# A contiguous buffer for the weights' shift, and another order of the first units' work, in a gated attention block with an MLP

## The chip, the cores and the metric

The kernel runs on one core of one Trainium2 chip. A core has five engines that each take their own instructions in order: TensorE (PE, matrix products; its weight loads are listed as PEld), VectorE (DVE), ScalarE (ACT), GpSimd (POOL) and SyncE (SP, which here only issues transfers). Sixteen DMA engines move data between the memory (DRAM) and the core's own memory (SBUF). Matrix products land in PSUM banks. The metric is the time of one execution on the device, in microseconds (us).

## The reference

Two blocks in a row. The first is a linear attention with a forget gate (4 batches, 8 heads, 768 steps, head size 48); the second is a layer norm and an MLP with ReLU and a residual (width 384, hidden 1536).

```python
f = 1.0 / (1.0 + np.exp(-f_logit))
for t in range(S):
    state = f[:, :, t, :, None] * state + np.einsum('bhd,bhe->bhde', k[:, :, t], v[:, :, t])
    y[:, :, t] = np.einsum('bhd,bhde->bhe', q[:, :, t], state)
...
x = np.ascontiguousarray(attn_out.transpose(0, 2, 1, 3)).reshape(B, S, H * D)
mu = np.mean(x, axis=-1, keepdims=True)
var = np.mean((x - mu) ** 2, axis=-1, keepdims=True)
xn = (x - mu) / np.sqrt(var + 1e-06) * g_ln
ch = np.maximum(xn @ w_ch1, 0.0) @ w_ch2
return (x + ch).astype(np.float32)
```

The MLP's weights arrive as 64-bit floats, all else as 32-bit floats. The kernel makes 32-bit floats of the weights itself.

## The kernel before

**Units and stages.** The 768 steps are cut into 12 units of 64 steps, all batches and heads together. A unit n has a list of attention stages, written a{n}.stage: gates (PE transposes f into a PSUM bank, ACT takes the sigmoid), after and upto (DVE scans with running products of the gates), kx (PE transposes k), k and q (DVE multiplies by the scans' results; q also transposes on PE), scores (PE), causal (DVE masks them), values (PE, and ACT copies the result to x), kt (PE transposes k back, ACT copies), chunk and state (the update of the state), stats and norm (DVE, with POOL for the root), turn (PE transposes the normed x, ACT multiplies by the gain into xt). For unit 0 most stages are done for two pairs of batches apart, with a 0 or 1 behind the name. Transposes and MLP products share four PSUM banks in turn; a bank is taken again when its last reader is done.

**The MLP.** Unit 0's first matrix product is done in steps h00 (first half of the tokens) and h01 (second half), six each; a step takes 256 of the 1536 hidden columns, 12 matmul instructions and a relu on ACT. So step i of h00 or h01 needs the weight piece i. For later units, and for the second product, the steps are named m{n}.

**The weights.** Both matrices are cut into six pieces each (w1: 256 columns of three row blocks; w2: two row blocks), 768 KB apiece as 64-bit words. A piece goes through four tokens of the list:

- f (line 513): SP issues its transfer into one of two "words" buffers.
- r (line 524): ACT reads the words twice, into "upper" (the high word, scaled; line 533) and into half of "units" (the low word; line 534).
- c (line 539): DVE clips "upper" (line 544) and shifts its bits by three (line 546). The shift writes straight to the piece's place in w1 or w2. In w1 that place is three runs of 256 elements out of rows of 1536; in w2 it is one run.
- w (line 550): ACT writes the signs into the other half of "units" (line 556), POOL adds "units" to the shifted words in place (line 557).

**The order.** START, a list of tokens written out by hand, gives the order in which the instructions of units 0 to 2 (and parts of 3 to 5) are put out; UNIT does the same for each later unit. As each engine works in order, the list sets the order on every engine and on the queues. Beside those above there are: l (load of f, q, k or v of a unit from SP's queue; L is the same from ACT's queue; a digit at the end is one of the two pairs of batches; a load of a pair is two transfers of 96 KB), p and P (splits into halves for transposing transfers, sent from POOL's or SP's queue), x (such a transfer), t, u and U (sums of weights, on DVE or POOL), and d (line 568: a matrix product of the identity with itself, into a bank that nobody reads).

The list is worked off by `run`:

```python
def run(plan):
    for token in plan.split():
```

Of the kernel before, what the change touches and what calls it, by code (L numbers as in the profile page):

```python
# [10 lines left out]
I32 = mybir.dt.int32  # L11
# [4 lines left out]
ALU = mybir.AluOpType  # L16
# [284 lines left out]


START = """
a0.gates0 l0q0 l0f1 f a0.after0 a0.carried l0k1 a0.upto0 l0k0 a0.gates1 a0.kx0 l0q1 f l0v0 l0v1 a0.after1 r c a0.upto1 a0.kx1 a0.k0 f a0.q0 a0.q1 w a0.scores0 a0.causal0 a0.k1 r f c w a0.values0 a0.kt a0.scores1 l1f a0.stats0 a0.causal1 r c d a0.norm0 l1q a0.chunk w a0.values1 a0.turn0 a0.stats1 r d a1.gates h00 c a0.norm1 a1.after w h00 a0.turn1 f f h00 r l1k a0.state h01 h01 h01 f a1.upto a1.kept c h00 a1.q w l1v r a1.kx a1.carried a1.k a1.scores a1.causal c r l2f w h00 f a1.values h01 a1.stats c l2k a2.gates f h01 r a1.kt h01 l3f l2q h00 a1.norm a1.turn a2.after f a2.kx w c a2.k P3f0 p3f1 a1.chunk w r l3k f r c a2.upto m1 a1.state f m1 m1 w P3k1 c m1 P3k0 w l3q a2.kept m1 t m1 r r x3f c l2v m1 w a3.gates a2.q L4f x3k a3.after c m1 a2.carried P3q1 a2.kt P3q0 w L4k a2.scores m0 P4f1 a2.causal m0 a2.values U a3.k P3K0 a2.stats u P4k1 a2.chunk m0 p4k0 x3q m0 U m0 a2.state a2.norm l4q a2.turn p3K1 a3.kept a3.upto L3v m0 P4f0 u l5f m2 a3.q t u x4f m2 m2 p4q0 P4q1 a3.kt a3.carried a3.scores a3.causal u t a4.gates x4k m2 m1 u a4.after u m2 m2 P5f0 p5f1 s2 a3.values a3.stats a3.norm l5k m1 U x4q P5k0 a3.chunk P5k1 m1 a4.upto a4.q l6f u l4v m2 l5v x5f m1 a4.k a3.turn a3.state u m2 P4K1 l5q m2 m2 a4.kept m2 u a5.gates p4K0 m2 U m2 y3
"""
UNIT = """
a{n}.kt a{n}.carried p{p}f1 a{o}.after a{n}.scores m{m} a{n}.causal m{m} m{m} m{m} P{o}q0 m{m}
# [8 lines left out]
def kernel(  # L316
# [19 lines left out]
    nc = tc.nc  # L336
    B, H, S, D = q.shape
    P = 128
# [38 lines left out]
    stage = changing.enter_context(tc.tile_pool(name="stage", bufs=2))  # L377
# [11 lines left out]
    for name in "fqk":  # L389
        t = consts.tile([P, G, H, 64], FP32, name=f"{name}raw")  # L390
# [120 lines left out]
    fetched, opened, clipped = [], [], []  # L511
# [27 lines left out]
    def clip():  # L539

        if not opened:
            return
        upper, units, to, name, r, w = opened.pop(0)
        nc.vector.tensor_scalar(out=upper, in0=upper, scalar1=-INF, scalar2=INF, op0=ALU.max,
                                op1=ALU.min)
        nc.vector.tensor_scalar(out=to.bitcast(I32), in0=upper.bitcast(I32), scalar1=3,
                                scalar2=None, op0=ALU.logical_shift_left)
        clipped.append((upper, units, to))

    def write():  # L550

        if not clipped:
            return
        upper, units, to = clipped.pop(0)
        signs = units.bitcast(F16).rearrange("p r (f two) -> p two r f", two=2)[:, 1]
        nc.scalar.activation(out=signs, in_=upper, func=AF.Copy)
        nc.gpsimd.tensor_tensor(out=to.bitcast(I32), in0=to.bitcast(I32), in1=units, op=ALU.add)

# [529 lines left out]
    def run(plan):  # L1090
        for token in plan.split():
# [8 lines left out]
            elif kind == "m":  # L1100
                if token not in running:
                    running[token] = mlp(int(rest))
                next(running[token])
            elif kind in "lL":
                queues = (nc.scalar if kind == "L" else nc.sync,)
                if rest[-1].isdigit():
                    load(int(rest[:-2]), rest[-2], (int(rest[-1]),), queues)
                else:
                    load(int(rest[:-1]), rest[-1], engines=queues)
            elif kind in "pP":  # L1110
                split(int(rest[:-2]), rest[-2], int(rest[-1]),
                      nc.sync if kind == "P" else nc.gpsimd)
            elif kind == "x":
                transfer(int(rest[:-1]), rest[-1])
            elif kind == "h":
                if token not in running:
                    running[token] = first_half(int(rest[0]), int(rest[1]))
                next(running[token])
            elif kind == "s":
                sums(int(rest))  # L1120
            elif kind == "y":
                if FIRST <= int(rest) < NU:
                    sums_of_x(int(rest))
            else:
                {"r": read, "c": clip, "w": write, "f": fetch, "t": mix, "d": idle,
                 "T": lambda: mix(nc.gpsimd), "u": mix_step,
                 "U": lambda: mix_step(nc.gpsimd)}[token]()
# [3 lines left out]
    for m in range(3, NU):  # L1131
# [4 lines left out]
        if m == NU - 2:  # L1136
# [5 lines left out]
                                    op=ALU.min)  # L1142
            nc.vector.tensor_scalar(out=small, in0=least_one, scalar1=LEAST, scalar2=None,
                                    op0=ALU.is_lt)
# [37 lines left out]
```

## Time and profile before

| | us |
|---|---|
| median of 3 runs | 434.26 |
| lowest, highest | 433.57, 434.93 |
| the profiled execution, its own time | 433.42 |
| its span, first to last instruction | 431.6 |
| PE idle in the span | 19.0 |

The granted TensorE clock is 1.00 in every stretch of the profile. In rows of the timeline, the first number is the start in us from the span's start, the second the duration in us; then engine, line, operation, what is written and what is read, shapes and types, how many instructions were merged, and in brackets the idle time before them with what ended it. A name such as SPq or ACTq is the engine's instruction queue, where transfers are issued. In rows by stage, a stretch is followed by the busy time of PE, PEld, DVE, ACT and POOL, the granted clock, the share of the DMA engines' time that was busy, and GB/s.

### The profile page before, as it was taken

How to read it: one execution, taken by the hardware profiler on the slowest of the kernel's cores; microseconds unless marked ns; L12 is line 12 of the kernel's file. 1: busy time of each engine (PE TensorE's matmuls, PEld its weight loads, DVE VectorE, ACT ScalarE, POOL GpSimd, SP SyncE). 2: the span in 40 equal slices, each digit the busy share in tenths (PEclk: the TensorE clock that was granted, in tenths of full speed). 3: DMA queues.
4: the chain of work that ended last, by engine and by line, in shares of the span. 5: the costliest groups of instructions: out<-in, count | busy, mean ns of one | idle time of the engine just before them, and what ended most of it. 6: DMA issues, size and time to landing. Idle time of an engine off the chain costs nothing.

```text
span 431.6 us, 12917 instructions
## 1 busy us (share of the span) xinstructions
PE 412.6 (96%) x5421; PEld 385.8 (89%) x5421; DVE 322.9 (75%) x505; ACT 227.7 (53%) x376; POOL 118.1 (27%) x153
## 2 busy tenths in 40 slices
PE   2799999999999999999999999999999999999995
PEld 1689987668779999989999999999999999999995
DVE  5679757684787879869879879879879879665561
ACT  2597888564252574563573573564673552351320
POOL 3355343421032115016116016016016015012021
PEclk9999999999999999999999999999999999999999
DMA  7999998969677697797697797698695781301001
GB/s 159 242 238 198 224 263 236 183 161 237 166 185 156 179 215 179 191 208 178 179 223 187 186 226 173 167 212 202 163 245 139 171 150 45 92 2 28 12 9 33
DMA packets 167839, 71.68 MB, mean 166 GB/s; under 512 B 151760, under 2 KB 157840, under 8 KB 167776
## 3 DMA queue, kind: packets, MB, share of 16 engines
q1 hardware_dynamic: 153248, 55.56, 59.1%
q0 software_dynamic: 3632, 11.85, 7.7%
q10 hardware_dynamic: 10896, 3.40, 4.2%
q8 instruction: 44, 0.72, 0.7%
q14 instruction: 19, 0.16, 0.1%
HBM read 28.31 MB, written 23.59 MB: 120 GB/s over the span
## 4 chain that ended last, share of the span: by engine, by line
PE 94%; SPq 1%; DMA 1%; DVE 1%; ACT 1%; issue 1%
PE pp L1040 32%; PE bx L940 11%; PE by L940 10%; PE po L1021 7%; PE ph L1011 7%; PE ph L889 4%; PE bz L940 4%; PE shared L760 3%; PE py L746 3%; PE py L796 3%; PE bw L940 2%; PE tr L654 2%; PE xp L875 2%; PE bv L940 2%; PE shared L834 2%; DMA kraw<-in_k_dram 1%
## 5 line engine op out<-in xcount | busy, mean ns | idle before, releaser
L951 ACT ACTIVATE h<-h 128x512 f32<-128x512 f32 x45 | 28.4, 631 | 42.2 <-DVE h L948 33.2
L1040 PE MATMUL pp<-mixed,h 128*128 128x192 f32 x240 | 42.3, 326 | 0.0
L1040 PE MATMUL pp<-w,h 128*128 128x192 f32 x240 | 40.8, 326 | 0.0
L1040 PE MATMUL pp<-mixed,s 128*128 128x192 f32 x240 | 40.6, 326 | 0.0
L1040 PEld LDWEIGHTS pp<-mixed,s 128*128 128x128 f32 x240 | 39.3, 190 | 0.0
L1040 PEld LDWEIGHTS pp<-mixed,h 128*128 128x128 f32 x240 | 39.1, 190 | 0.0
L1040 PEld LDWEIGHTS pp<-w,h 128*128 128x128 f32 x240 | 38.8, 190 | 0.3
L877 ACT ACTIVATE xt<-xp,gain 128x128 f32<-128x128 f32 x72 | 20.1, 380 | 30.7 <-PE xp L875 30.6
L948 DVE TENSOR_TENSOR h<-h,bx 128x512 f32<-128x512 f32 x36 | 24.6, 683 | 15.3 <-PE bx L940 15.3
L427 ACT COPY Kplanes<-kh 128x1024 uint16<-128x1024 uint16 x18 | 18.2, 1046 | 32.6 <-DVE kh L708 27.3
L1021 PE MATMUL po<-w,h 128*128 128x384 f32 x96 | 32.9, 490 | 0.0
L662 DVE TENSOR_TENSOR_SCAN after<-gates,ends 128x1040 f32<-128x1040 f32 (+1 forms) x13 | 28.8, 2216 | 4.8 <-ACT gates L691 3.1
L1011 PE MATMUL ph<-xt,w 128*128 128x256 f32 x144 | 31.9, 380 | 0.0
L1011 PEld LDWEIGHTS ph<-xt,w 128*128 128x128 f32 x144 | 27.2, 190 | 4.2
L673 DVE TENSOR_TENSOR_SCAN upto<-gates,starts 128x1040 f32<-128x1040 f32 (+1 forms) x13 | 30.5, 2349 | 0.4
L940 PE MATMUL bx<-y,v 128*128 128x128 f32 x216 | 28.5, 275 | 0.0
L1021 PEld LDWEIGHTS po<-w,h 128*128 128x128 f32 x96 | 17.7, 190 | 10.7
L940 PEld LDWEIGHTS bx<-y,v 128*128 128x128 f32 x216 | 26.3, 192 | 0.0
L822 POOL TENSOR_SCALAR rstd<-mv 128x2 f32<-128x2 f32 (+1 forms) x13 | 8.0, 615 | 66.4 <-DVE mv L820 66.2
L427 ACT COPY fplanes<-fraw 128x1024 uint16<-128x1024 uint16 x18 | 18.8, 1053 | 9.1 <-DMA kraw<-in_k_dram 4.2
L427 ACT COPY kplanes<-kraw 128x1024 uint16<-128x1024 uint16 x18 | 18.1, 1044 | 6.6 <-DMA kraw<-in_k_dram 5.0
L1040 PE MATMUL pp<-w,s 128*128 128x192 f32 x120 | 21.1, 326 | 0.0
(166 smaller groups left out, 934.0 us busy)
## 6 DMA issues: line engine op xcount, KB each, us to landing
w_0words<-in_moe_w_ch_dram SPq DMA_DIRECT2D x7, 768.0 KB, 6.1
kraw<-in_k_dram SPq DMA_DIRECT2D x44, 96.0 KB, 4.8
v<-in_v_dram SPq DMA_DIRECT2D x44, 96.0 KB, 3.9
Khalves<-Kplanes POOLq DMA_DIRECT2D x16, 256.0 KB, 3.6
fhalves<-fplanes POOLq DMA_DIRECT2D x14, 256.0 KB, 4.2
kraw<-in_q_dram SPq DMA_DIRECT2D x36, 96.0 KB, 3.2
khalves<-kplanes SPq DMA_DIRECT2D x11, 256.0 KB, 2.5
qhalves<-qplanes SPq DMA_DIRECT2D x10, 256.0 KB, 3.8
```

The costliest lines, as they stand in the source:

```text
L427: nc.scalar.copy(out=to, in_=src)
L662: nc.vector.tensor_tensor_scan(out=at["after"].rearrange(flat)[:, c0:c1][:, ::-1], data0=gt[:, c0 + 1:c1 + 1][:, ::-1], data1=ends.rearran ...
L673: nc.vector.tensor_tensor_scan(out=at["upto"].rearrange(flat)[:, c0:c1], data0=gt[:, c0:c1], data1=starts.rearrange(flat)[:, c0:c1], initi ...
L746: nc.tensor.matmul(py[half(b ^ r), r, e * D:(e + 1) * D], lhsT=qh[head_rows(r), 2 * e + b], rhs=kept[head_rows(r), b, e], start=e == 0, st ...
L877: nc.scalar.mul(out=xt[:, m, g * P:(g + 1) * P], in_=pt[:, m], mul=gain[:, m:m + 1])
L889: nc.tensor.matmul(ph[:, j], lhsT=w1[:, m, (i + j) * P:(i + j + 1) * P], rhs=xt[:, m, tokens], start=m == 0, stop=m == KD - 1)
L940: nc.tensor.matmul(banks[bank][:, i], lhsT=right[:, i * P:(i + 1) * P], rhs=left, start=new and i == 0, stop=True, skip_group_check=True)
L948: nc.vector.tensor_tensor(out=out[to], in0=out[to], in1=bank, op=op)
L951: nc.scalar.activation(out=out[to], in_=out[to] if bank is None else bank, func=AF.Relu)
L1011: nc.tensor.matmul(ph[:, j], lhsT=w1[:, m, (i + j) * P:(i + j + 1) * P], rhs=xt[:, m], start=m == 0, stop=m == KD - 1)
L1021: nc.tensor.matmul(po, lhsT=h[:, i, g * P:(g + 1) * P], rhs=w2[:, i], start=i == 0, stop=i == KF - 1)
L1040: nc.tensor.matmul(pp, lhsT=a[:, i], rhs=b[:, i], start=i == 0, stop=i == KH - 1)
```

## The change

The shift writes to a tile "body" of its own, one buffer of 128 x 768 words, and POOL reads it from there:

```diff
@@ clip
-        nc.vector.tensor_scalar(out=to.bitcast(I32), in0=upper.bitcast(I32), scalar1=3,
-                                scalar2=None, op0=ALU.logical_shift_left)
-        clipped.append((upper, units, to))
+        body = stage.tile([P, r, w], I32, tag="body", bufs=1, name=f"{name}body")
+        nc.vector.tensor_scalar(out=body, in0=upper.bitcast(I32), scalar1=3, scalar2=None,
+                                op0=ALU.logical_shift_left)
+        clipped.append((upper, units, body, to))
@@ write
-        upper, units, to = clipped.pop(0)
+        upper, units, body, to = clipped.pop(0)
...
-        nc.gpsimd.tensor_tensor(out=to.bitcast(I32), in0=to.bitcast(I32), in1=units, op=ALU.add)
+        nc.gpsimd.tensor_tensor(out=to.bitcast(I32), in0=body, in1=units, op=ALU.add)
```

START is replaced by another order of nearly the same tokens: 256 in place of 251. Five are d (seven in place of two), two u became U, and ten transfers changed their queue. In the file each list is one line; here the beginnings are broken into several, up to where both have named h00 four times and h01 three times:

```diff
-a0.gates0 l0q0 l0f1 f a0.after0 a0.carried l0k1 a0.upto0 l0k0 a0.gates1 a0.kx0 l0q1 f
-l0v0 l0v1 a0.after1 r c a0.upto1 a0.kx1 a0.k0 f a0.q0 a0.q1 w a0.scores0 a0.causal0
-a0.k1 r f c w a0.values0 a0.kt a0.scores1 l1f a0.stats0 a0.causal1 r c d a0.norm0 l1q
-a0.chunk w a0.values1 a0.turn0 a0.stats1 r d a1.gates h00 c a0.norm1 a1.after w h00
-a0.turn1 f f h00 r l1k a0.state h01 h01 h01 f a1.upto a1.kept c h00 a1.q w l1v r a1.kx
-a1.carried a1.k a1.scores a1.causal c r l2f w h00 f a1.values h01
...
+a0.gates0 a0.after0 f L0k0 d a0.upto0 l0f1 l0k1 a0.gates1 a0.kx1 l0q1 r d l0q0
+a0.carried a0.after1 a0.kx0 a0.upto1 f l0v0 a0.k1 d c f a0.k0 d d w a0.q1 a0.q0 L0v1
+a0.scores0 a0.causal0 l1f a0.scores1 r c w a0.values0 a0.causal1 a0.kt a0.stats0 r c
+a0.norm0 w a0.values1 a0.stats1 a0.turn0 f f d r d a1.gates c w l1k l1q f h00 a0.norm1
+a0.chunk a0.turn1 r a0.state h00 l2f h01 a1.after h01 c f h00 w h01 h00 a1.upto a1.kept
+a1.q a1.kx l1v a1.k r f a1.carried a1.scores c a1.causal w r c h00 h01 a1.values
...
```

The load of f's first pair for unit 0 stands ahead of both lists, one transfer on SP's queue and one on ACT's.

More of the change, by code (lines that the diff above doesn't have):

```diff
@@ L303 @@
 START = """
-a0.gates0 l0q0 l0f1 f a0.after0 a0.carried l0k1 a0.upto0 l0k0 a0.gates1 a0.kx0 l0q1 f l0v0 l0v1 a0.after1 r c a0.upto1 a0.kx1 a0.k0 f a0.q0 a0.q1 w a0.scores0 a0.causal0 a0.k1 r f c w a0.values0 a0.kt a0.scores1 l1f a0.stats0 a0.causal1 r c d a0.norm0 l1q a0.chunk w a0.values1 a0.turn0 a0.stats1 r d a1.gates h00 c a0.norm1 a1.after w h00 a0.turn1 f f h00 r l1k a0.state h01 h01 h01 f a1.upto a1.kept c h00 a1.q w l1v r a1.kx a1.carried a1.k a1.scores a1.causal c r l2f w h00 f a1.values h01 a1.stats c l2k a2.gates f h01 r a1.kt h01 l3f l2q h00 a1.norm a1.turn a2.after f a2.kx w c a2.k P3f0 p3f1 a1.chunk w r l3k f r c a2.upto m1 a1.state f m1 m1 w P3k1 c m1 P3k0 w l3q a2.kept m1 t m1 r r x3f c l2v m1 w a3.gates a2.q L4f x3k a3.after c m1 a2.carried P3q1 a2.kt P3q0 w L4k a2.scores m0 P4f1 a2.causal m0 a2.values U a3.k P3K0 a2.stats u P4k1 a2.chunk m0 p4k0 x3q m0 U m0 a2.state a2.norm l4q a2.turn p3K1 a3.kept a3.upto L3v m0 P4f0 u l5f m2 a3.q t u x4f m2 m2 p4q0 P4q1 a3.kt a3.carried a3.scores a3.causal u t a4.gates x4k m2 m1 u a4.after u m2 m2 P5f0 p5f1 s2 a3.values a3.stats a3.norm l5k m1 U x4q P5k0 a3.chunk P5k1 m1 a4.upto a4.q l6f u l4v m2 l5v x5f m1 a4.k a3.turn a3.state u m2 P4K1 l5q m2 m2 a4.kept m2 u a5.gates p4K0 m2 U m2 y3
@@ new lines @@
+a0.gates0 a0.after0 f L0k0 d a0.upto0 l0f1 l0k1 a0.gates1 a0.kx1 l0q1 r d l0q0 a0.carried a0.after1 a0.kx0 a0.upto1 f l0v0 a0.k1 d c f a0.k0 d d w a0.q1 a0.q0 L0v1 a0.scores0 a0.causal0 l1f a0.scores1 r c w a0.values0 a0.causal1 a0.kt a0.stats0 r c a0.norm0 w a0.values1 a0.stats1 a0.turn0 f f d r d a1.gates c w l1k l1q f h00 a0.norm1 a0.chunk a0.turn1 r a0.state h00 l2f h01 a1.after h01 c f h00 w h01 h00 a1.upto a1.kept a1.q a1.kx l1v a1.k r f a1.carried a1.scores c a1.causal w r c h00 h01 a1.values a1.stats l2k h01 a1.kt a2.gates r l3f h01 a1.norm a1.chunk h00 f a1.turn f a2.after a2.kx w P3f0 a2.k m1 a1.state l2q r c w p3f1 l3k f c w m1 r f c m1 P3k1 a2.upto l2v m1 P3k0 l3q m1 w r r c w a2.kept x3f m1 m1 P3q1 t m1 a3.gates a2.q l4f x3k c m0 a2.kt P3q0 w p4f1 a3.after a2.carried L4k a2.scores a2.causal m0 a3.k U a2.values m0 a2.chunk a2.stats a2.state u P3K0 P4k1 x3q p4k0 a2.norm m0 m0 p3K1 a2.turn a3.upto u a3.kept l4q m0 U a3.q L3v t p4f0 U p4q0 m2 m2 a3.carried L5f a3.scores a3.causal U U a3.kt x4f t x4k m2 m2 u a3.values p4q1 u m1 l5k P5f0 m1 a3.chunk a4.gates u U a4.after p5f1 a3.stats l4v x4q m2 m2 a3.norm s2 m1 m2 p5k0 m2 L6f a3.turn a4.upto m1 a4.k a4.q P5k1 m2 l5v a3.state x5f a4.kept y3 P4K1 P4K0 l5q m2 u m2 a5.gates m2 u m2
```

## The prediction

> **What bounds the kernel now.** I read first the page's busy times, then busy times by stage, then the waits of TensorE (PE), then the timeline of the first 40 us.
>
> ```profile
> span 431.6 us, 12917 instructions
> PE 412.6 (96%) x5421; PEld 385.8 (89%) x5421; DVE 322.9 (75%) x505; ACT 227.7 (53%) x376; POOL 118.1 (27%) x153
> 40.00:50.00 10.00, 9.33 (x204) 8.97 (x197) 6.30 (x13) 7.10 (x13) 3.87 (x4) 1.00 0.95 172
> 50.00:160.00 110.00, 110.00 (x1335) 90.49 (x1334) 78.69 (x108) 64.56 (x98) 28.57 (x30) 1.00 0.86 203
> 160.00:200.00 40.00, 39.19 (x513) 38.50 (x512) 34.04 (x53) 21.75 (x35) 12.76 (x17) 1.00 0.86 192
> PE tr L654 <- DMA fraw<-in_f_logit_dram: 6.2, 2, 4.6
> PE tr L654 <- DMA kraw<-in_k_dram: 4.8, 1, 4.8
> ```
>
> The stage rows give, behind the stretch, busy us of PE, its weight loads, DVE (VectorE), ACT (ScalarE) and POOL (GpSimd), then the granted clock, the DMA share and GB/s. PE is busy 412.6 of 431.6 us: 19.0 us are idle. From 50 to 160 us it is never idle; 40 to 50 has 0.67 us, 160 to 200 has 0.81. Most of the rest lies in front, where PE waits for f and k (6.2 and 4.8 us). So only the front can be changed by much, and I judge the new list by one question: **when has PE finished the same set of work as before**, from the first gates through the four h00 steps and three h01 steps (weight pieces 0 to 3). After it PE has no idle time in which a delay could be recovered, but the two gaps named.
>
> The rows of the front (start, duration):
>
> ```profile
> 7.25 1.09 PE L654 MATMUL tr<-ident,fraw 128*128 128x128 f32 x4 [1.57 <-DMA fraw<-in_f_logit_dram]
> 8.37 0.60 ACT L691 ACTIVATE gates<-tr 128x512 f32<-128x512 f32 x1 [2.00 <-PE tr L654]
> 9.08 1.22 DVE L662 TENSOR_TENSOR_SCAN after<-gates,ends 128x520 f32<-128x520 f32 x1
> ...
> 12.08 0.56 DVE L544 TENSOR_SCALAR w_0upper<-w_0upper 128x768 f32<-128x768 f32 x1 [1.78 <-ACT w_0upper L533]
> 12.67 0.95 DVE L546 TENSOR_SCALAR w<-w_0upper 128x768 int32<-128x768 int32 x1
> 13.15 1.94 PE L654 MATMUL tr<-ident,kraw 128*128 128x128 f32 x8 [4.82 <-DMA kraw<-in_k_dram]
> 13.77 1.24 DVE L673 TENSOR_TENSOR_SCAN upto<-gates,starts 128x520 f32<-128x520 f32 x1
> 16.73 0.92 ACT L533 ACTIVATE w_256upper<-w_256words 128x768 f32<-128x768 f32 x1 [2.82 <-DMA w_256words<-in_moe_w_ch_dram]
> 16.73 1.13 PE L760 MATMUL shared<-qh,kh 48*64 48x64 f32 x32
> 17.93 0.69 DVE L772 TENSOR_TENSOR sc<-shared,causal 128x512 f32<-128x512 f32 x1 [0.40 <-PE shared L760]
> 18.53 0.68 DVE L680 TENSOR_TENSOR kh<-tr,after 128x512 f32<-128x512 f32 x1
> 18.63 0.37 SPq L521 DMA_DIRECT2D w_768words<-in_moe_w_ch_dram  x1
> 19.71 1.97 PE L787 MATMUL kp<-ident,kh 128*128 128x128 f32 x8
> 21.63 1.07 ACT L789 COPY kt<-kp 128x512 f32<-128x512 f32 x2
> 22.59 0.92 ACT L533 ACTIVATE w_512upper<-w_512words 128x768 f32<-128x768 f32 x1
> 23.61 0.93 PE L834 MATMUL shared<-v,kt 64*48 64x48 f32 x63 [0.29 <-ACT w_512upper L533]
> 24.31 1.08 ACT L556 ACTIVATE w_512units<-w_512upper 128x768 f16<-128x768 f32 x1
> 25.23 0.33 ACT L805 COPY x<-py 128x192 f32<-128x192 f32 x1
> 25.54 0.55 PE L875 MATMUL xp<-ident,xn 128*128 128x128 f32 x3 [0.36 <-DVE xn L864]
> 26.24 0.89 ACT L877 ACTIVATE xt<-xp,gain 128x128 f32<-128x128 f32 x3
> 27.00 0.92 ACT L533 ACTIVATE w_768upper<-w_768words 128x768 f32<-128x768 f32 x1
> 28.73 1.08 ACT L691 ACTIVATE gates<-tr 128x512 f32<-128x512 f32 x2
> 29.67 0.42 ACT L891 ACTIVATE h<-ph 128x256 f32<-128x256 f32 x1
> 30.39 6.89 PE L889 MATMUL ph<-xt,w 128*128 128x128 f32 x60
> 37.12 1.04 PE L654 MATMUL tr<-ident,qraw 128*128 128x128 f32 x8
> ```
>
> Neighbours overlap a little, so ACT's prices are taken from start to start: a kt copy pair 0.96 (21.63 to 22.59), reading a piece 1.73 (22.59 to 24.31), a signs step 0.92, the x copies 1.0, three xt multiplies 0.76, the two sigmoids 0.94, a relu 0.3 to 0.4. Sixty matmul rows are five h steps: 30.39 to 37.12, 6.73 us, 1.35 a step. 37.12 is when the old list has finished the set.
>
> **The shift.** Into w1 (rows of 256 inside rows of 1536) it takes 0.95; into w2, where two rows are contiguous, 0.56:
>
> ```profile
> 48.21 0.56 DVE L546 TENSOR_SCALAR w<-w_0upper 128x768 int32<-128x768 int32 x1
> 65.61 1.98 POOL L557 TENSOR_TENSOR w<-w,w_0units 128x768 int32<-128x768 int32 x1 [4.06 <-ACT w_0units L556]
> 65.96 2.06 DVE L546 TENSOR_SCALAR w<-w_0upper 128x768 int32<-128x768 int32 x1
> ```
>
> The new buffer is contiguous, so I take 0.56 for the six w1 pieces: 0.39 less each, 2.3 us of DVE in all; the bounds are 0 (if it stays 0.95) and 2.3. Little of it is on the path: signs needs only the clip, and DVE has room. POOL's add keeps its 1.98. One buffer adds a wait: the shift of a piece waits until POOL has added the one before. In the list c and w alternate, and in the working below the adds of the first three pieces are over more than 1 us before the next shift, that of the fourth about when the next one is due; I take 0, with 1 us as the other end. Where an add is late, DVE stands, and the scans, causal masks and norms queue behind it. The third row shows another price: a shift of the fast kind that began inside an add took 2.06 instead of 0.56, ending about 0.4 us after it. So a collision costs up to 1.5 us.
> The Trainium skill, page "SBUF — State Buffer", section "Who interferes with whom", says that a VectorE operation in a two-port mode and a GpSimd operation exclude each other for a whole instruction. By that rule, the slow shifts were immune and the six fast ones can now be blocked. With every one blocked the sum would rise by 9 us of DVE; the row at 65.96 agrees.
>
> **The loads.** On SP's queue the order was f0, q0, f1, piece 0, k1, k0, q1, piece 1, v; it becomes f0, piece 0, f1, k1, q1, q0, piece 1, v0, piece 2, unit 1's f, then pieces 3 and 4. k0 and v1 go to ACT's queue: two issues each; k0's stand behind the first sigmoid and ahead of the second; v1's stand ahead of reading piece 1.
>
> ```profile
> DMA packets 1531, 0.51 MB, mean 255 GB/s; under 512 B 1417, under 2 KB 1417, under 8 KB 1530
> DMA packets 1265, 0.24 MB, mean 118 GB/s; under 512 B 1265, under 2 KB 1265, under 8 KB 1265
> DMA packets 355, 0.70 MB, mean 350 GB/s; under 512 B 13, under 2 KB 13, under 8 KB 355
> w_768words<-in_moe_w_ch_dram SPq DMA_DIRECT2D x1, 768.0 KB, 6.2
> ```
>
> Those are 22 to 24, 24 to 26 and 18 to 20 us: 2 us move 1265 to some 1531 small packets, or about 355 large ones. A load of 96 KB is 64 tokens by 8 heads, 512 packets: 0.67 to 0.8 us; a piece is 3 rows on 128 partitions, 384 packets, 2.2 us. Piece 0 in the place of two q loads puts f1 later by 2.2 − 1.3 to 1.6: 0.6 to 0.9, up to 1.5 where a piece is slower. I take 0.95: f1 at **8.2**. All twelve loads and piece 0 are the same sum as before, so piece 1 lands as before, at 16.7 where ACT had waited for it, and the last of q one piece earlier, about 14. Piece 3 was issued at 18.63 and landed 6.2 later, 24.8, ahead of unit 1's f; now four loads of f stand ahead of it: +2.6 to +3.2, less what v1 on the other queue and the fuller start give back, an estimate of 0 to 1.5 (v1 is two loads, 1.3 to 1.6). Bounds 25.9 to 28.0; I take **26.8**.
>
> **The path, step by step** (DVE first). f1 8.2; sigmoid 9.3; scan after from 10.0 (the distances of the rows from 7.25 to 9.08); reciprocal and scan upto from 11.3; k1 12.7; clip and shift 13.3 to 14.4; k0 15.0; q1 and q0, if PE has them ready, to 16.4. PE from k1's landing (f1's 8.2 and two loads, 9.8): two sets of four k transposes, four idle products, eight q transposes. An idle product streams as many columns as four transposes, so these are eight groups of four; eight transposes took 1.94 at 13.15 and 1.04 at 37.12. The granted clock is 1.00 in every row above, so the page doesn't show the cause of this doubling. All eight groups slow: 7.8 us, q0 ready at 17.6; fast from the fifth on: 15.8. I take 16.2, q0's product done and scores0 at **17.0** (bounds 16.4 and 18.4). The mask follows by the product's time, 0.75 at the fast rate (1.13 at the slow one); then mask and clip, 0.6 each from start to start: signs of piece 1 at 17.0 + 0.75 + 1.2 = 18.95.
>
> From there ACT has no pause: signs 0.92, x 0.98, kt 0.96, read piece 2 1.73, signs 0.92, x 0.98, xt 0.76: **26.2**. Read piece 3 waits for 26.8 (0.6 lost): 28.5; sigmoids 29.5; signs 30.4; relu 30.7; xt of the second half, first part at 31.0. PE beside it: turn0 at 24.3 (behind statistics and norm on DVE and POOL), 0.55; two idle products and a1's gates, 2 × 0.5 + 1.0, so h00 at 26.7; chunk (0.93; before it was done ahead, at 23.61), turn1, h00: 26.7 + 1.35 + 0.9 + 0.5 + 1.35 = 30.8. So the first h01 step starts at 31.1, and the five steps (two h01, h00, h01, h00) end the set at **37.8**: 0.7 us behind the old 37.1. Without the wait for piece 3 it would start at 30.8 and end at 37.5.
>
> Behind it the old list loses 0.67 us between 40 and 50 us, where its only order is scores, one h step, values; the new one has two h steps between scores and values. I count 0.4 of it back. The other edits (queues of the splits for units 3 to 5, two more mixing steps on POOL) lie under a PE that has no idle time: 0, with 0.8 either way. **Sum: +0.7 − 0.4 = +0.3.** The profiled execution is 433.42, 1.8 over its span and 0.84 below the median of 434.26; a difference is carried to the median: **434.6 us**.
>
> **Rivals.**
> *Slower, by piece 3.* Unit 1's f delays piece 3; ACT stands in front of it with sigmoids, signs and xt behind. It decides from a landing at 26.2 on, and each us is a us at h01. At 28.5 ACT is 2.3 late, xt at 32.7, the set ends at 39.4: 39.4 − 37.1 − 0.4 = +1.9, **436.2**. For it: four loads at 0.65 to 0.8. Against: the slow queue is relieved of v1 and k0.
> *Faster, by a filled PE.* The idle products keep PE running from 9.8 on, the doubling comes by 13.3, scores0 is bound by DVE at 16.4, piece 3 lands by 26: the set ends 0.6 ahead of 37.5, at 36.9: −0.2 − 0.4 = −0.6, and both idle stretches (0.67 and 0.81) may go whole: −1.7, **432.6**. For it: before, PE was busy with gaps from 13.15 and eight transposes still took 1.97 at 19.71; the gaps are filled now. Against: ACT's chain behind the scores is the same length either way.
>
> The Trainium skill, page "TensorE: Matmul & The Clock Gate", section "What's actually happening", has the array at half rate until about one window of 3.4 us has been busy. By that rule the doubling falls at 13.2 to 16.6 us here and this rival has its chance; the trace agrees in that the transposes were still slow at 19.71, after the gaps, and fast at 37.12.
> *A collision or the single buffer.* A fast shift ahead of the norms meets an add: 1.5 us each; two on the path: 0.3 + 3.0 = +3.3, **437.6**.
> *The shift stays at 0.95.* Of DVE's 2.3 us only those ahead of scores0 and the first norm lie on the path, 0.4 at most: +0.7, 435.0.
>
> **How the numbers follow.** About 0.3% (1.3 us) is what a measurement can tell from no change. Forecast 0.40, slower by piece 3 0.23, faster 0.26, collision 0.06, unchanged shift 0.05. The faster rival's spread just reaches the bound, the forecast's own bounds (f1, scores, piece 3) spill a little on each side: faster 0.27, same 0.44, slower 0.29. The forecast's own range is 433.3 to 435.9; with the rivals' prices, leaving out most collisions and the best of the faster case, 431.8 to 437.2.
>
> **What would show it.** L546 at 0.56 for all pieces. Second f transposes near 8.2. The first masked scores near 17.8. The read of the fourth piece at 26 to 27, with a wait for DMA ahead of it. The first h01 near 31, the eight q transposes of unit 1 near 38. A first h01 before 30 speaks for the faster rival, one after 32 for the slower. PE idle beyond 50 us of more than 1.5 us would make the reckoning itself wrong, since it holds that only the front counts.

## The result and the profile after

The kernel after takes **439.49 us** (median of 20 runs, 436.00 to 442.84) beside 434.28 us before (20 runs): a ratio of 1.0101, 95% interval 1.0075 to 1.0127. It is 1% slower; the forecast was 434.6, no change, with a range that ended at 437.2. The profiled execution took 438.46 us with a span of 436.8, 5.2 us more than the 431.6 of before.

The head of the page of after:

```profile
span 436.8 us, 12950 instructions
PE 416.5 (95%) x5431; PEld 388.9 (89%) x5431; DVE 321.1 (74%) x502; ACT 227.9 (52%) x376; POOL 118.3 (27%) x159
```

PE is idle for 20.3 us, 1.3 more than before, and busy for 3.9 us more. So most of the 5.2 us are not a new wait: the same products, and a few idle ones, took longer. Busy times by stage say where it is not:

```profile
50.00:160.00 110.00, 109.94 (x1268) 90.21 (x1268) 78.23 (x105) 62.95 (x97) 31.50 (x36) 0.99 0.81 189
160.00:200.00 40.00, 40.00 (x649) 39.34 (x648) 32.21 (x52) 24.30 (x41) 9.99 (x15) 1.00 0.87 200
```

From 50 to 200 us PE has no idle time to speak of. The timeline of PE in the front of after, in the columns of before:

```profile
9.60 1.08 PE L655 MATMUL tr<-ident,fraw 128*128 128x128 f32 x4 [3.22 <-DMA fraw<-in_f_logit_dram]
10.47 1.06 PE L655 MATMUL tr<-ident,kraw 128*128 128x128 f32 x4
...
14.00 1.09 PE L655 MATMUL tr<-ident,kraw 128*128 128x128 f32 x4 [1.62 <-DMA kraw<-in_k_dram]
14.88 2.63 PE L571 MATMUL idle<-ident 128*128 128x256 f32 x6
17.35 1.04 PE L655 MATMUL tr<-ident,qraw 128*128 128x128 f32 x8
19.33 0.69 PE L761 MATMUL shared<-qh,kh 48*64 48x64 f32 x32 [0.94 <-DVE qh L681]
...
26.86 0.52 PE L876 MATMUL xp<-ident,xn 128*128 128x128 f32 x3 [2.95 <-DVE xn L865]
27.21 1.64 PE L571 MATMUL idle<-ident 128*128 128x256 f32 x4
28.64 1.91 PE L655 MATMUL tr<-ident,fraw 128*128 128x128 f32 x8
30.35 1.77 PE L890 MATMUL ph<-xt,w 128*128 128x128 f32 x12
...
41.34 1.04 PE L655 MATMUL tr<-ident,qraw 128*128 128x128 f32 x8
...
46.83 0.38 PE L761 MATMUL shared<-qh,kh 48*64 48x64 f32 x9 [1.68 <-issue]
```

The set that the prediction used as its yardstick ends at 41.34 (before 37.12): **4.2 us late**. Three pieces can be read off. The first scores come 2.6 us later (19.33, before 16.73), although turn0 (the three products at 26.86) is only 1.3 late. From turn0 to the f transposes of unit 1 pass 1.78 us in place of 0.81 (one of the two idle products there is new), and those transposes last 1.91, against 1.08 in this row of before's timeline:

```profile
26.35 1.08 PE L654 MATMUL tr<-ident,fraw 128*128 128x128 f32 x8
```

So a second thing happens behind the norm: PE is slow again. Busy times by stage, cut on the grid of 3.41 us on which the granted clock changes:

```profile
20.66:24.08 3.42, 2.85 (x104) 2.44 (x104) 2.50 (x6) 2.75 (x6) 1.64 (x1) 1.00 1.06 162
24.08:27.49 3.41, 0.64 (x5) 0.64 (x6) 1.51 (x3) 3.39 (x7) 1.48 (x4) 1.00 0.52 159
27.49:30.90 3.41, 3.41 (x15) 3.03 (x14) 2.09 (x5) 3.38 (x8) 2.39 (x3) 0.50 1.04 288
30.90:34.32 3.42, 3.42 (x88) 3.25 (x87) 2.49 (x2) 2.46 (x7) 1.98 (x1) 1.00 1.48 156
44.56:47.97 3.41, 1.73 (x57) 1.53 (x48) 1.64 (x3) 2.77 (x3) 1.82 (x1) 1.00 1.03 280
47.97:51.38 3.41, 3.41 (x18) 3.41 (x18) 1.53 (x3) 0.38 (x1) 0.00 (x0) 0.50 0.83 100
```

The clock (the third number from the end) goes to 0.50 twice, each time for 3.41 us, right behind a stretch of 3.41 us in which PE was busy for 0.64 and 1.73 us. A halved stretch does 1.7 us less work, so the two put 3.4 us on PE's busy time. The 3.9 us by which it grew are a balance: five more idle products add about 2.2 us (one takes 0.43 at full speed, from 25.92 to 26.35 in before), and an earlier full clock takes some back.

For the record of the clock begins only with its first change to full speed, at 17.25 in after and at 22.52 in before. Ahead of it the clock column reads 1.00 as well, but there eight transposes of before take 1.91 to 1.97 us, the slow rate. So "the granted clock is 1.00", in the prediction and ahead of it, reads a stretch without a record: before ran slow up to 22.52. Behind that its clock is not halved again in its profile.

What the first half of the front waits for is in the chain of work that ended last (start, duration), cut to its first 15 us:

```profile
1.64 7.16 DMA w_0words<-in_moe_w_ch_dram
...
8.82 0.63 ACTq L462
...
9.49 4.38 DMA kraw<-in_k_dram
```

The issue of k0 on ACT's queue follows the landing of weight piece 0, a transfer that it has nothing to do with. The timeline of ACT and the other engines in after, for that and for the prediction's other marks:

```profile
5.62 0.60 ACT L692 ACTIVATE gates<-tr 128x512 f32<-128x512 f32 x1 [2.54 <-PE tr L655]
8.82 1.32 ACTq L462 DMA_DIRECT2D kraw<-in_k_dram  x2
...
28.51 0.90 ACT L533 ACTIVATE w_768upper<-w_768words 128x768 f32<-128x768 f32 x1
```

The first sigmoid starts at 5.62; k0, the next on this queue, leaves at 8.82. The operands of the issues in the trace give the reason (start, duration, queue, the semaphore waited for, the semaphore that its landing raises):

```
1.64 0.85 SP  -                  104   weight piece 0
1.66 0.57 ACT -                  105   gain
2.54 0.63 SP  -                  106   f1, first half
5.24 3.16 SP  waits for 100      100   q1, first half
8.82 0.63 ACT waits for 104      104   k0, first half
9.49 0.65 ACT waits for 106      106   k0, second half
```

Eight semaphores (100, 102 and 104 to 109) go round among the transfers in about the order of their issue, whatever the queue. A transfer that gets one already in use is issued only when the earlier transfer has landed. In the new list k0 got the one of piece 0, 768 KB, which landed at 8.80. (The 3.16 us of q1's issue are not such a wait: its semaphore was free at 3.77. What held it the trace does not tell.)

The shift behaves as foreseen. The instructions of its line in after (count, then shortest, median and longest in ns), and what DVE waited for ahead of it:

```profile
L547 DVE TENSOR_SCALAR w_0body<-w_0upper x7: 560/561/561, 15.2 to 86.1; 128x768 int32<-128x768 int32 x7
L547 DVE TENSOR_SCALAR w_256body<-w_256upper x1: 559/559/559, 21.4 to 21.4; 128x768 int32<-128x768 int32 x1
...
  POOL w L558: 3.2, 1
```

All take 0.56 us, and none was held up by an add of POOL. Three clips of pieces that began inside such an add took 1.53 to 2.08 us in place of 0.56, but between 63 and 80 us, where PE has no idle time. The single buffer made DVE wait once, for 3.2 us, and no engine waited for that shift.

### The profile page after: what moved, and what is told of

Same layout as the page of the kernel before. It is cut to its first block, busy times and chain, and to the rows that moved or that the text cites. A ratio compares the mean times of both kernels' runs of the same rounds, so it can differ in the third digit from the quotient of the medians.

```text
span 436.8 us, 12950 instructions
## 1 busy us (share of the span) xinstructions
PE 416.5 (95%) x5431; PEld 388.9 (89%) x5431; DVE 321.1 (74%) x502; ACT 227.9 (52%) x376; POOL 118.3 (27%) x159
## 4 chain that ended last, share of the span: by engine, by line
PE 94%; DMA 3%; DVE 1%; ACT 1%; issue 1%; SPq 0%; ACTq 0%; DVEq 0%
PE pp L1041 31%; PE bx L941 11%; PE by L941 10%; PE ph L1012 7%; PE po L1022 7%; PE ph L890 4%; PE bz L941 4%; PE py L797 3%; PE py L747 3%; PE shared L761 3%; PE bw L941 2%; PE shared L835 2%; PE xp L876 2%; PE bv L941 2%; PE tr L655 2%; DMA w_0words<-in_moe_w_ch_dram 2%
## 5 line engine op out<-in xcount | busy, mean ns | idle before, releaser
L674 DVE TENSOR_TENSOR_SCAN upto<-gates,starts 128x1040 f32<-128x1040 f32 (+1 forms) x13 | 28.1, 2158 | 0.4
L428 POOL DMA_DIRECT2D qhalves<-qplanes x9 | 4.9, 546 | 63.6 <-ACT qplanes L427 63.6
L427 ACT COPY qplanes<-kraw 128x1024 uint16<-128x1024 uint16 x18 | 18.7, 1039 | 5.2 <-DMA out_dram<-x 3.8
```

Of the source, the lines that this page charges most:

```text
L427: nc.scalar.copy(out=to, in_=src)
L674: nc.vector.tensor_tensor_scan(out=at["upto"].rearrange(flat)[:, c0:c1], data0=gt[:, c0:c1], data1=starts.rearrange(flat)[:, c0:c1], initi ...
```

## The experiments

My theory after the two traces: the list alone costs the time, by a late k0 and by PE's clock falling back behind an idle stretch. Rivals: the second half of f, 2.35 us later than before (9.60, before 7.25); the idle products put on the path; the buffer. All kernels were run beside the kernel before, whose median in those sessions was 434.3 to 435.1; so compare the ratios, not the medians. "Set" is the start of the q transposes of unit 1 in the profiled execution, "halved" the time at half clock behind the first full one, up to 60 us, in it.

| kernel | median us (runs) | ratio to before, 95% interval | set | halved |
|---|---|---|---|---|
| before | 434.28 (20) | 1 | 37.12 | 0 |
| after | 439.49 (20) | 1.0101 (1.0075 to 1.0127) | 41.34 | 6.8 |
| shift_only | 434.08 (12) | 0.9990 (0.9961 to 1.0020) | 37.04 | 0 |
| order_only | 439.52 (7) | 1.0093 (1.0050 to 1.0136) | 43.96 | 6.8 |
| piece0_behind_f1 | 435.53 (12) | 1.0022 (0.9989 to 1.0055) | 41.78 | 6.8 |
| piece0_first | 434.52 (12) | 1.0001 (0.9963 to 1.0038) | 38.51 | 6.8 |
| k0_on_sp | 435.78 (10) | 1.0030 (0.9991 to 1.0068) | 39.73 | 6.8 |
| other_semaphore | 437.06 (12) | 1.0043 (1.0011 to 1.0075) | 40.15 | 6.8 |
| filled_gap | 436.20 (12) | 1.0037 (1.0009 to 1.0064) | 39.09 | 3.4 |
| no_idle_before_q | 438.82 (7) | 1.0104 (1.0061 to 1.0146) | 42.01 | 0, but full only from 31.90 |
| chunk_first | 437.53 (10) | 1.0078 (1.0043 to 1.0113) | 41.08 | 3.4 |
| k0_on_sp_filled | 435.87 (12) | 1.0014 (0.9980 to 1.0049) | 40.15 | 0 |
| mended | 437.14 (12) | 1.0049 (1.0019 to 1.0079) | 40.59 | 3.4 |
| mended_piece3 | 434.45 (6) | 0.9991 (0.9955 to 1.0027) | 38.65 | 0 |

One profiled execution is not the median: those of piece0_behind_f1, piece0_first, other_semaphore and mended_piece3 lay 1.1 to 2.8 us above theirs, that of filled_gap 1.6 below. So verdicts go by the ratios, and the profiles show mechanisms. Every run also lists its mean recorded clock, which misses only what lies ahead of the first full clock; its means over all runs of a kernel are used below.

**The buffer or the list.** *shift_only* has the new buffer with the old list, *order_only* the new list with the old shift.

```diff
 shift_only (against after)
-START = the new list
+START = the old list
 order_only (against before)
-START = the old list
+START = the new list
```

> The new buffer for the shift with the old list. The shift into the buffer takes 0.56 us for all twelve pieces instead of 0.95 for six. If the loss is all in the list (my theory): within 0.3% of before, PE idle about 19 us, the same work done (37.1 us at the first q transposes of unit 1) up to 0.5 us earlier. If the buffer itself costs (a wait of the shift for POOL's add, or collisions): slower by 1 us or more, with a wait of DVE for POOL at the shift.

> The new list with the old shift into the weights' place. If the loss is all in the list: 438 to 441 us, as the changed kernel, or 0.4 to 1 us more, as the six shifts cost 0.39 us each again on DVE. If the buffer costs: nearer to before, 435 to 437.

The buffer alone changes nothing that can be measured (0.9990), the list alone costs what the change costs (1.0093 beside 1.0101). DVE had room for 0.39 us in each piece; that it has less to do is worth nothing where PE and ACT set the path.

**Piece 0's place.** *piece0_behind_f1* is after with piece 0 behind f's second half; *piece0_first* is shift_only with piece 0 right behind f's first half, the old list otherwise.

```diff
 piece0_behind_f1
-a0.gates0 a0.after0 f L0k0 d a0.upto0 l0f1 l0k1
+a0.gates0 a0.after0 L0k0 d a0.upto0 l0f1 f l0k1
 piece0_first
-a0.gates0 l0q0 l0f1 f a0.after0
+a0.gates0 f l0q0 l0f1 a0.after0
```

> The changed kernel with the transfer of piece 0 behind f's second pair, as in the old list, and all else as changed. Theory (late landings): f's second transposes start near 7.3 instead of 9.6 us, k's first pair no longer has to wait for the landing of piece 0 before ACT's queue issues it (8.8 in the changed kernel) and its transposes start near 12 instead of 14.0, the first scores come 1.5 to 2 us earlier, and the time falls by 1.5 to 2 us. Rival (the list behind the loads is what costs: idle products, the gap before the first norm): the loads land earlier but the time falls by less than 0.7 us.

> The new buffer, the old list, and only the transfer of piece 0 moved to right behind f's first pair. Theory (late landings): f's second transposes at 9.5 instead of 7.3, k at 13 as before since the same bytes stand ahead of it, the DVE scans later, the first scores up to 1 us later, 0 to 1.5 us slower than before. Rival (an early piece fills the DMA engines sooner): not slower, up to 0.5 us faster.

PE in the timeline of piece0_first:

```profile
10.86 1.09 PE L655 MATMUL tr<-ident,fraw 128*128 128x128 f32 x4 [5.41 <-DMA fraw<-in_f_logit_dram]
13.19 1.94 PE L655 MATMUL tr<-ident,kraw 128*128 128x128 f32 x8 [1.24 <-DMA kraw<-in_k_dram]
```

There f's second half is 3.6 us later than before, more than in after, and the time is that of before (1.0001): k comes at the same 13.2 as in before, and what is late hides behind it. So in the old list a late f1 costs nothing; in the new one k0_on_sp, with f1 at 9.27, speaks against it too. But after with piece 0 moved back is better by about 0.8%, so piece 0 does harm in the new list by another way. Its profile does not show which: k0 leaves at 5.82, not 8.82, but lands only 0.5 us earlier (13.35, in after 13.87), scores0 starts at 18.95, and the clock is halved twice.

**The late k0.** *k0_on_sp* puts k0 on SP's queue behind k1. *other_semaphore* keeps the list and adds one transfer of 12 bytes behind that of the gain, so that each later transfer takes the next semaphore.

```diff
 k0_on_sp
-f L0k0 d a0.upto0 l0f1 l0k1 a0.gates1
+f d a0.upto0 l0f1 l0k1 l0k0 a0.gates1
 other_semaphore
+    spare = consts.tile([1, KD], FP32, name="spare")
+    nc.scalar.dma_start(out=spare, in_=moe_g_ln[0:KD].rearrange("(o c) -> o c", o=1))
```

> The changed kernel with k's first pair on SP's queue, behind its second pair, instead of ACT's queue. Theory: k0 no longer waits for the landing of piece 0, its transposes start near 12.5 instead of 14.0, the first scores 1 to 1.5 us earlier, the time 0.5 to 1.5 us lower. Rival: the DMA engines are full either way, k0 lands no earlier, and the time is that of the changed kernel.

> The changed kernel with one tiny transfer more at the very start (12 bytes on ACT's queue behind the gain, to a tile nobody reads), and no other edit. The trace shows eight completion semaphores that the transfers take in turn, and k's first transfer of the first pair drew the one that piece 0 had, so that its issue waited for the landing of piece 0 (8.82 us). The extra transfer shifts the turn by one. If that wait is what costs (theory): ACT issues k's first pair right behind the first sigmoid, at 6 to 6.5 us, its transposes start near 12 instead of 14.0, and the time falls by 2 to 4 us, as when k's first pair went to SP's queue. If it was the queue and not the semaphore (the rival): the issue stays at 8.8 and the time at 439.

The issue of k0 in other_semaphore, from ACT's timeline:

```profile
5.72 3.84 ACTq L462 DMA_DIRECT2D kraw<-in_k_dram  x2
```

What differs is whose semaphore k0 takes, and its first half leaves at 5.72 in place of 8.82. That shows the wait. The second half now stands behind the landing of f1 and leaves at 8.96, so k0's transposes move only from 14.00 to 13.38; scores0 (19.45) are no earlier in this execution, in which the first full clock came at 18.46 (17.25 in after) and the q transposes took 1.84. So the better ratio (1.0043, with an interval that touches that of after) is not traced to them. PE in k0_on_sp:

```profile
12.23 0.85 PE L655 MATMUL tr<-ident,kraw 128*128 128x128 f32 x4
12.92 1.46 PE L571 MATMUL idle<-ident 128*128 128x256 f32 x6
14.43 1.09 PE L655 MATMUL tr<-ident,qraw 128*128 128x128 f32 x8
17.28 0.69 PE L761 MATMUL shared<-qh,kh 48*64 48x64 f32 x32 [1.76 <-DVE qh L681]
```

k0 is there without a wait at 12.23, scores0 start 2.0 us earlier than in after, and the set ends 1.6 earlier although the clock is halved as often. The ratio drops by 0.7%, about 3 us, more than I expected. This edit does two things, though: it takes the wait away, and it puts k0 ahead of the q loads on SP's queue, so that it lands at 11.58 in place of 13.87. How much of the gain is the semaphore and how much the place was not tried apart.

**The clock.** *filled_gap* is after with six more idle products ahead of turn0, where PE stood for 2.95 us; *chunk_first* fills the same stretch with real work, the chunk that the new list had moved behind turn0; *no_idle_before_q* takes away the three idle products between k and q.

```diff
 filled_gap
-a0.values1 a0.stats1 a0.turn0
+a0.values1 a0.stats1 d d d d d d a0.turn0
 chunk_first
-a0.stats1 a0.turn0 f f d r d a1.gates c w l1k l1q f h00 a0.norm1 a0.chunk a0.turn1
+a0.stats1 a0.chunk a0.turn0 f f d r d a1.gates c w l1k l1q f h00 a0.norm1 a0.turn1
 no_idle_before_q
-a0.k1 d c f a0.k0 d d w a0.q1
+a0.k1 c f a0.k0 w a0.q1
```

> The changed kernel with six more idle products (some 2.6 us of PE at full rate) in the stretch from 23.9 to 26.9 us in which PE waits for the first norm. Theory 1 (clock): that idle stretch is what halves the granted clock for the 3.4 us from 27.5; filled, the clock stays at 1.00 there, the eight f transposes of unit 1 take 1.0 instead of 1.9 us, and the time falls by about 1.7 us, although more work is done. Theory 2 (only the late chain counts, the clock follows of itself): no gain, or 0.5 us slower, as the products delay the norm's transposes.

> The changed kernel with unit 0's chunk (64 products, 0.87 us) moved ahead of the first normed transposes, into the stretch where PE waits for the norm. If only the moved work counts: 0.9 us faster than the changed kernel, the clock still halved behind the gap (2.1 us of it are left). If that much work already keeps the clock: 2 to 2.6 us faster.

> The changed kernel without the three idle products that stand between the second k transposes and the q transposes (2.6 us at half rate). Theory 2: the q transposes come 1.5 to 2.4 us earlier, the first scores at 17.5 instead of 19.3, and the time falls by 1.5 to 2 us. Theory 1: the clock rises later, scores and values at half rate eat 1 to 1.5 us of that, and a halved window may stand elsewhere: a gain of less than 1 us or none.

PE in filled_gap:

```profile
23.61 2.86 PE L571 MATMUL idle<-ident 128*128 128x256 f32 x12
26.31 0.49 PE L876 MATMUL xp<-ident,xn 128*128 128x128 f32 x3
...
27.50 1.04 PE L655 MATMUL tr<-ident,fraw 128*128 128x128 f32 x8
```

Work that nobody reads makes the kernel faster by about 0.6%, some 2.8 us: turn0 waits for nothing, and the f transposes are back at 1.04 us. From turn0 to the end of the set pass 12.78 us. In the four profiles with the same list behind turn0 and a halved stretch there (after, order_only, piece0_behind_f1, k0_on_sp) it is 14.43 to 14.48; in other_semaphore, which kept the clock there, 12.85. So a halved stretch behind turn0 costs the set 1.7 us. It holds beyond one execution: the mean recorded clock is 0.9963 over the 12 runs of filled_gap and 0.9894 over the 20 of after, which makes 3 us. With the chunk in the same place the gain is smaller and the intervals overlap (1.0078): PE still waited 1.5 us for the norm. Without the products ahead of q scores0 start 1.7 us earlier (17.62), and nothing is gained (1.0104). Why is in its busy times, cut at the same grid of 3.41 us:

```profile
14.83:18.25 3.42, 2.52 (x33) 2.12 (x36) 2.71 (x5) 2.22 (x3) 1.82 (x1) 1.00 1.14 253
18.25:21.66 3.41, 2.60 (x85) 2.32 (x78) 2.41 (x4) 1.83 (x3) 0.50 (x1) 1.00 1.37 217
21.66:25.07 3.41, 2.80 (x40) 2.31 (x39) 0.94 (x3) 3.08 (x7) 2.11 (x3) 1.00 0.83 198
25.07:28.49 3.42, 1.85 (x6) 1.70 (x7) 2.06 (x5) 3.36 (x9) 1.71 (x1) 1.00 0.63 165
28.49:31.90 3.41, 3.41 (x16) 3.12 (x16) 1.82 (x4) 3.15 (x5) 1.20 (x3) 1.00 1.30 260
```

The clock column reads 1.00 here only because the record begins with the first change, at 31.90; the transposes and scores in these stretches last 1.91 and 1.13 us, the slow rate. Stretches in which PE was busy for 2.5 to 2.8 of 3.41 us did not bring the full clock; one filled whole did. So the idle products on the path buy the clock and cost about what they buy.

**Both mended.** *k0_on_sp_filled* is k0_on_sp with five idle products ahead of turn0; *mended* is k0_on_sp with the chunk and three idle products there, and without the two around unit 1's gates.

```diff
 k0_on_sp_filled (against k0_on_sp)
-a0.stats1 a0.turn0
+a0.stats1 d d d d d a0.turn0
 mended (against k0_on_sp)
-a0.stats1 a0.turn0 f f d r d a1.gates
+a0.stats1 d d a0.chunk d a0.turn0 f f r a1.gates
...
-h00 a0.norm1 a0.chunk a0.turn1
+h00 a0.norm1 a0.turn1
 mended_piece3 (against mended)
-a0.causal0 l1f a0.scores1 r c w a0.values0
+a0.causal0 a0.scores1 r f l1f c w a0.values0
...
-a0.turn0 f f r a1.gates
+a0.turn0 f r a1.gates
```

> Both mends at once: k's first pair on SP's queue, and five idle products in the stretch where PE waits for the first norm. If the late k and the halved clock are two separate costs: 1 to 2 us below k's pair on SP's queue alone (435.8), so 434 to 435. If the halved clock came only from the late k: the time of that kernel or up to 0.5 us more.

> A version meant to beat both: k's first pair on SP's queue, unit 0's chunk and three idle products in the stretch before the first norm, and the two idle products behind it taken out. By the theory the set of work up to the q transposes of unit 1 ends near 36.5 us (39.7 with k on SP's queue, less 1.7 for one halved window, 0.9 for the chunk, 0.5 to 0.9 for the two products), the rest takes 393 to 394.5 as in the other runs: 431.5 to 433.5 us, 0.2 to 0.6% faster than before. If PE isn't what the front waits for: 434 to 435, as before.

The gains do not add, and both kernels missed what I expected: 1.0014 and 1.0049, not the 0.997 that the two savings would give from 1.0101. The intervals of k0_on_sp and k0_on_sp_filled overlap so far that no gain of the filling is shown there. In k0_on_sp_filled the clock is full from 15.80 on, and the set still ends at 40.15. The timeline of mended, ACT and PE:

```profile
29.42 0.92 ACT L533 ACTIVATE w_768upper<-w_768words 128x768 f32<-128x768 f32 x1 [0.32 <-DMA w_768words<-in_moe_w_ch_dram]
...
32.04 0.55 PE L876 MATMUL xp<-ident,xn 128*128 128x128 f32 x3 [1.65 <-DVE xn L865]
```

The fourth weight piece (piece 3, w_768) is read at 29.42, as soon as it has landed. DVE's clip of it stands ahead of the second norm, which turn1 waits for. In k0_on_sp_filled the same rows stand at 28.99 with a wait of 1.39 for the transfer, and at 31.69 with 1.19 for the norm. That is the prediction's rival "slower, by piece 3": unit 1's f goes ahead of it. The last kernel, *mended_piece3*, moves only transfers: piece 3 goes back ahead of unit 1's f.

> In the kernel called mended, the fourth weight piece was issued at 24.05 us, behind unit 1's loads of f, and ACT could read it only at 29.42; the second norm stood behind it on DVE and turn1 waited for it (1.65 us). Here its transfer goes ahead of unit 1's f, as in the list before the change; one idle product pair stays as it was. If the landing of this piece is what binds in mended: the piece is read at 26.5 to 27 without a wait for the transfer, the wait of turn1 for the norm is gone or under 0.5, the set (start of the q transposes of unit 1) ends at 37 to 38.5, and the time is 433 to 434.5 us, about that of the kernel before. If something else binds (the clock halved before the first norm, or ACT's own work): the set stays at 39.5 to 40.6 and the time at 436 to 437. If unit 1's f now comes too late in its turn: the transposes of f start later than 28.5 and the wait of PE for them appears, with a time above 436.

The timeline of mended_piece3, SP's queue, ACT and PE:

```profile
20.43 0.37 SPq L521 DMA_DIRECT2D w_768words<-in_moe_w_ch_dram  x1
...
27.50 0.90 ACT L533 ACTIVATE w_768upper<-w_768words 128x768 f32<-128x768 f32 x1
...
30.11 0.54 PE L876 MATMUL xp<-ident,xn 128*128 128x128 f32 x3
...
38.65 1.04 PE L655 MATMUL tr<-ident,qraw 128*128 128x128 f32 x8
```

The piece leaves at 20.43 in place of 24.05, is read at 27.50 without a wait for its transfer, and turn1 waits for nothing at 30.11. The set ends 1.9 us earlier than in mended and the ratio falls from 1.0049 to 0.9991, the kernel before. Three things missed what I expected: the read is at 27.50, not 26.5 to 27, since ACT gets there only then; the set is at 38.65, above 38.5; and PE now waits 0.71 and 0.46 us for unit 1's f.

So the wait for piece 3 is shown, but not that it made the gain. Of the 1.9 us, 1.7 lie ahead of turn0 (27.69 in mended, 26.02 here), where the clock was halved in the profile of mended and not in this one; behind turn0 12.90 us became 12.63. Over all runs the mean recorded clock is 0.9938 in mended and 0.9982 here, which makes 1.9 of the 2.5 us between the two ratios. Why the clock holds better in this kernel stays open. No kernel of the study is shown to beat the one before.

## Why the prediction was wrong

**What held.** Only the front counts: PE's idle time from 50 to 200 us is 0.06 us, so a delay of the front is carried to the end; the idle stretch of 0.81 behind 160 us did go, as the faster rival had it, but by luck: such stretches come and go from kernel to kernel (last section). The shift takes 0.56, costs and gains nothing, and neither the collision nor the single buffer showed on the path. Piece 1 is read at 16.71 (forecast 16.7), and piece 3 landed at 26.37 (forecast 26.8).

**The step that failed first: "k0's stand behind the first sigmoid and ahead of the second".** The prediction took that as the whole condition of k0's issue, near 6.2 us. It left at 8.82, held by the landing of piece 0. The eight groups of four that were to run "from 9.8" began at 10.47 and stood 1.62 us for k0, so that q's transposes ran to 18.4 in place of 16.2 and scores0 started at 19.33 in place of 17.0, beyond the bound of 18.4. The first full clock, which the faster rival put at 13.3, came at 17.25. In k0_on_sp, where PE does not stand for k0, it came at 12.74, and scores0 started at 17.28. The trace of before could have warned: there, too, each transfer from the ninth on takes a semaphore used before, but those of its first ones belonged to small early loads, which had landed before their turn, so nothing was held; I read the rows of the queues without their operands.

**The term that was missing: the clock can fall again.** The prediction asked when PE's clock would double, never whether it would halve. The new list moves the chunk behind turn0 and, with the norm 1.3 us later, leaves PE with 2.95 us of nothing ahead of it; the stretch behind runs at half speed. In the set that shows as the f transposes (1.91 for 1.08), the idle products behind turn0 and the first h00 step. The row for the chunk, "before it was done ahead, at 23.61", was used for its 0.93 us only.

**f1** was mis-sized: forecast 8.2, measured 9.60. By its semaphores f1 landed at 9.46 in after, at 7.11 in before and at 5.65 in piece0_behind_f1, where neither piece 0 nor q stands ahead of it. So the q loads cost 1.5 us, as the prediction had it, but piece 0 cost 3.8, not 2.2. piece0_first shows that this is worth nothing by itself.

**The 0.4 us counted back between 40 and 50 us** did not come: PE stood 1.68 us there, in before 0.67. The prediction took that idle time for a matter of the list's order; the traces speak for the loading of PE's instructions (last section). The second halving falls behind this stop.

**Piece 3** was read at 28.51 without a wait, since ACT came there 2.3 us late. So the rival "slower, by piece 3" didn't act in after, though its sign came true: the first h01 step, named as slower if after 32, began at about 34.6 (one step of 1.34 behind 33.30). In mended the piece did make PE wait, 1.65 us.

**How the 1% divides** can be read off for the set of the two profiled executions: of its 4.2 us, about 1.3 are the later turn0 (what is left of the late scores0), 1.7 the halved stretch behind it, 0.9 the chunk, which now stands behind turn0 (32.05 to 32.91), and 0.4 the idle product that is new there. For the median it can be bounded, not settled. The mean recorded clock over the 20 runs of after is 0.9894, which makes 4.6 us of lost clock in a span of 437; over the 25 runs of before beside shift_only it is 0.9957, 1.9 us, so that the clock of before, too, falls again in most of its runs. That is 2.8 us more, or 1.6 halved stretches of 1.7 us. Were all of it on the path, it would be 2.8 of the 4.4 us that the ratio stands for, and the late k0, the idle products and the later chunk the rest. Against it stands the slow time ahead of the first full clock, which no run records and which was 5.3 us shorter in the profile of after. Repairs agree in size (k0_on_sp about 3 us, filled_gap about 2.8) but overlap: an earlier k0 also changes which stretches PE fills. What piece0_behind_f1 gained by stays open.

The Trainium skill, page "TensorE: Matmul & The Clock Gate", section "What's actually happening", says that the window of 3.4 us runs freely and that one idle window throttles the array. The trace agrees on the window (3.41 us, on one grid within an execution). It differs on "idle": windows in which PE was busy for 0.64 and for 1.73 of 3.41 us were both followed by half speed.

## What to carry to other kernels

Reordering a front that is bound by latency moves PE's idle time about; ask of each new gap whether the clock survives it, not only what it delays. Before a transfer moves to another queue, or a large one to the head of the list, look whose completion semaphore it takes: a queue that seems free can be held by a transfer on another one. And when two repairs do not add, look for what was late behind them, and at the clock of each run; here a transfer that the first two delays had hidden became a wait, and the clock differed as well.

## What was not expected of the hardware

- The granted clock changes only on a grid of 3.41 us, and it follows PE's busy time in the stretch before, though not by one threshold. Of the full-speed stretches of the front in these 14 profiles, all in which PE was busy for at most 36% were followed by a halved one, and none with 74% or more; between 41% and 72% both happened (54% kept the clock in after, 72% lost it in other_semaphore). From half speed, stretches with 74 to 82% did not bring the full clock in no_idle_before_q, and those with 88% and more did, but for one in piece0_first (100%), behind which a second halved one came.
- The grid stands otherwise against the kernel's start in each profile (a change at 17.25 in after, at 19.76 in filled_gap). So the same idle gap may fall into one stretch or across two. That this makes runs of one kernel differ fits the spread of after's runs (436.0 to 442.8, at clocks of 0.985 to 0.994) but wasn't tried apart.
- An issue on ACT's queue waited 3.1 us for a transfer of SP's queue that happened to hold the same one of eight completion semaphores; a transfer of 12 bytes put elsewhere in the order released it.
- Loading of PE's own instructions seems to stop PE. In 12 of the 14 profiles PE stands for 0.36 to 1.68 us ahead of the 470th to 472nd of its products, with no semaphore that ends it ("issue"), whatever the list has there: 45.15 in after, 43.54 in k0_on_sp, 41.03 in shift_only. Each of these stops ends 2.3 to 3.2 us after the start of a packet of 16 KB on a DMA queue that the page lists as "instruction". filled_gap and mended_piece3 have none. The 0.81 us in which PE stood behind 160 us in before end in the same way, 2.8 us after such a packet. No run tried it apart.
